# The first weight matrix moves to GpSimd's DMA queue, as one load, and the planner gives way to written order lists

## The chip, the cores and the metric

The kernel runs on one core of a Trainium2 chip. A core has five engines that run side by side, each through a program of its own: TensorE (matmuls and weight loads), VectorE, ScalarE, GpSimd and SyncE (here it only issues DMA transfers). They wait for one another by semaphores. Data come from HBM into SBUF by DMA; an engine that issues a DMA goes on with its program, and whoever needs the data waits for the DMA's semaphore. Matmul results go to PSUM. The metric is the device time of one execution in microseconds, the median of several runs.

## What is computed

An MLP mixer block over 2048 tokens of 512 features, in bfloat16:

```python
h = gelu(layernorm(x) @ w1)                  # x [2048, 512], w1 [512, 512]
# the four feature quarters of h are shifted along the tokens by +1, -1, +2, -2 (zeros come in)
hs = shifted(h) @ w2                         # w2 [512, 512]
x1 = x + hs
out = x1 + gelu(layernorm(x1) @ w3) @ w4     # w3 [512, 1792], w4 [1792, 512]
```

The layer normalizations have no learned scale; gelu is the tanh approximation.

## The kernel before

The tokens are 16 tiles of 128. All weights and activations stay in SBUF, so each is loaded once. For each tile `t` of layer 1: row statistics (either `bnst`/`bnag` on VectorE, lines 432 and 434, or two sums on ScalarE, lines 411 and 416), the reciprocal root `rstd` on GpSimd (line 439), the normalized rows into `xn_buf` (lines 448, 461, 470, 473), the transpose to `xnT` (on TensorE for the first tiles, line 506, with a copy out of PSUM on line 514; by a transposing DMA on SyncE's queue for the others, line 479), the first product with w1 (`up1`, line 642) and its gelu (line 657), the product with w2 (`mix`, line 697), whose shift is an offset in the columns of `hT`, and the addition to x (lines 709 and 713). Layer 2 then goes the same way with w3 (`up2`, line 642) and w4 (`down`, line 731), the last addition (line 739) and the store.

Tile 0 is special. Its rows are only centered (line 448, in two halves), transposed (line 506), and multiplied with w1 as rows (`rows0`, line 544, in two steps of two chunks of 128 features each); the gelu (line 585) applies the scale, and the result is transposed back (line 610). The first step, `rows0_0`, reads chunks 0 and 1 of w1, the second, `rows0_1`, chunks 2 and 3.

Before the first real matmul TensorE runs nine matmuls on zeros (line 756). ScalarE runs one small gelu (line 764) on the constant `eps_c`, ahead of its first row sum. GpSimd starts with eight small instructions that make constants (lines 364 to 374): the fixed columns of the statistics, the exponent for the reciprocal root, the identity matrix for the transposes, `eps_c`, and the zero edges of `hT`.

Every step is an `Op` with an engine, the resources that it reads and writes, and an estimated duration `dur`. TensorE's order is the string `SCRIPT`. `LOADS` is the order of the loads, all on SyncE; there w1 comes as two loads, `w1a` (chunks 0 and 1) and `w1b` (2 and 3), behind tiles 0-1 and 2 of x. For everything else, `order` works out due times from the durations, with corrections in `BIAS`, and `place` simulates the engines and the DMA rings to choose each engine's next step. `emit` then writes the programs in this order, with the semaphore waits that the resources ask for. Instructions up to the last one that the simulation starts before `ENTRY` are put ahead of the engines' wait in the start barrier.

Of the kernel before, what the change touches and what calls it, by code (L numbers as in the profile page):

```python
# [6 lines left out]
P = 128  # L7
# [7 lines left out]
class Op:  # L15


    def __init__(self, name, eng, fn, reads, writes, dur, queue):
        self.name, self.eng, self.fn = name, eng, fn
        self.reads, self.writes = list(reads), list(writes)  # L20
        self.dur, self.queue = dur, queue
        self.idx = 0
        self.descs = 8.0
        self.prio = 1e9
        self.first = None

class Program:

    HOP = {"pe": 200.0, "dve": 155.0, "act": 220.0, "pool": 120.0, "sp": 70.0}
    LOOK = {"dve": 300.0, "act": 300.0}
    DUE = 179877.0
    BEGIN = {"sp": 30.0, "act": 150.0, "pe": 400.0, "dve": 150.0, "pool": 450.0}
    ENTRY = 1900.0
    COLD, RESTART = 4300.0, 800.0
    RING = 150.0
    LAG = {"load": 750, "tp": 350}

    def __init__(self):  # L40
        self.ops = []
        self.lines = []

    def add(self, eng, name, fn, reads=(), writes=(), dur=100.0, queue=None):
        op = Op(name, eng, fn, reads, writes, dur, queue)
        op.idx = len(self.ops)
        self.ops.append(op)
        return op

    def line(self, names):  # L50

        self.lines.append(list(names))

    def order(self):
# [25 lines left out]
        order_only = set()  # L80
        for names in self.lines:
            for a, b in zip(names, names[1:]):
                assert named[a].eng == named[b].eng, (a, b)
                order_only.add((named[a].idx, named[b].idx))
        last = None
        pe_pos = 0
        for op in self.ops:
            if op.eng == "pe":
                if last is not None:
                    preds[op.idx].add(last.idx)  # L90
                last = op
                op.prio = pe_pos
                pe_pos += 1
        order_only = {(a, b) for a, b in order_only if a not in preds[b]}
        for a, b in order_only:
            preds[b].add(a)
        succs = [set() for _ in self.ops]
        for i, d in enumerate(preds):
            for j in d:
                succs[j].add(i)  # L100
        left = [len(s) for s in succs]
        stack = [i for i, n in enumerate(left) if n == 0]
        seen = 0
        while stack:
            i = stack.pop()
            seen += 1
            for j in preds[i]:
                if self.ops[j].eng != "pe":
                    self.ops[j].prio = min(self.ops[j].prio, self.ops[i].prio)
                left[j] -= 1  # L110
                if left[j] == 0:
                    stack.append(j)
        assert seen == len(self.ops), "cycle"
        if self.DUE:

            topo, left = [], [len(d) for d in preds]
            stack = [i for i, n in enumerate(left) if n == 0]
            while stack:
                i = stack.pop()
                topo.append(i)  # L120
                for j in succs[i]:
                    left[j] -= 1
                    if left[j] == 0:
                        stack.append(j)
            due, t = {}, self.DUE
            for op in self.ops:
                if op.eng == "pe" and not op.name.startswith("warm"):
                    due[op.idx] = t
                    t += op.dur
            for i in reversed(topo):  # L130
                op = self.ops[i]
                late = due.get(i, 1e9)
                for j in succs[i]:
                    o = self.ops[j]
                    hop = 70.0 if op.queue else (self.HOP[op.eng] if o.eng != op.eng else 120.0)
                    work = (2300.0 if op.queue == "tp" else op.dur + 1850.0) if op.queue else op.dur
                    late = min(late, o.prio - hop - work)
                op.prio = late
        for op in self.ops:
            op.prio += BIAS.get(op.name, 0.0)  # L140
            if op.first is not None:
                op.prio = op.first
        for names in self.lines:
            for a, b in reversed(list(zip(names, names[1:]))):
                named[a].prio = min(named[a].prio, named[b].prio - 1e-3)

        self.preds = preds
        out = self.place(succs, order_only)
        for a, b in order_only:
            preds[b].discard(a)  # L150
        return out

    def place(self, succs, order_only):

        npend = [len(d) for d in self.preds]
        ready = [0.0] * len(self.ops)
        cands = {e: [] for e in ENGINES}
        for op in self.ops:
            if npend[op.idx] == 0:
                cands[op.eng].append(op)  # L160
        free = dict(self.BEGIN)
        rings = {"sp": [], "act": []}
        fed = {}
        clock = moved = last = turned = self.total = 0.0
        out = []

        def finish(limit):
            nonlocal clock
            while True:
                heads = {e: r[0] for e, r in rings.items() if r}  # L170
                if not heads:
                    return None
                live = [e for e in heads if heads[e][0] <= clock]
                later = min([h[0] for h in heads.values() if h[0] > clock], default=1e18)
                if not live:
                    if later > limit:
                        return None
                    clock = later
                    continue
                first = min(live, key=lambda e: heads[e][1])  # L180
                step = heads[first][1] * len(live)
                ends = clock + step <= min(later, limit)
                if not ends:
                    step = min(later, limit) - clock
                for e in live:
                    heads[e][1] -= step / len(live)
                clock += step
                if ends:
                    return rings[first].pop(0)[2]
                if clock >= limit:  # L190
                    return None

        def release(op, o, at):
            npend[o.idx] -= 1
            if at is not None:
                ready[o.idx] = max(ready[o.idx], at)
            if npend[o.idx] == 0:
                cands[o.eng].append(o)

        def land(op):  # L200
            nonlocal moved, last, turned
            if op.queue == "tp":
                turned = max(clock + 500.0, op.start + 2450.0, last + 500.0, turned + 480.0)
                at = turned + self.LAG["tp"]
            elif op.name.startswith("out"):
                at = clock + 300.0
                self.total = max(self.total, at)
            else:
                moved += op.dur
                at = clock + 600.0 + min(600.0, 0.3 * moved) + (600.0 if op.dur > 1400.0 else 0.0)  # L210
                at += 50.0 if moved <= 1200.0 else self.LAG["load"] - 300.0 if moved <= 4000.0 else self.LAG["load"] if moved <= 11000.0 else self.LAG["load"] + 650.0
            if op.queue != "tp":
                last = max(last, at)
            op.landed = at
            for j in succs[op.idx]:
                if (op.idx, j) not in order_only:
                    release(op, self.ops[j], at + 30.0)

        while len(out) < len(self.ops):
            while True:  # L220
                best = None
                for e in ENGINES:
                    if cands[e]:
                        t = max(free[e], min(ready[o.idx] for o in cands[e]))
                        if best is None or t < best[0]:
                            best = (t, e)
                op = finish(best[0] if best else 1e17)
                if op is None:
                    break
                land(op)  # L230
            t, e = best
            look = self.LOOK.get(e, 1.0)
            op = min((o for o in cands[e] if ready[o.idx] <= t + look), key=lambda o: (o.prio, o.idx))
            cands[e].remove(op)
# [674 lines left out]
```

## Time and profile before

| | |
|---|---|
| median of 3 runs | 135.35 us (135.31 to 135.44) |
| span of the profiled execution | 133.7 us |
| what lies around the span (median less span) | 1.6 us |
| TensorE busy | 130.6 us, 98% of the span |
| TensorE's first real matmul (transposes of tile 0) | 4.24 us |
| first weight load of `rows0` | 5.40 us |
| loads from HBM | 6.82 MB |

The profiled execution's own time is its span, first to last instruction; the runs' time has the start and end of the program around it. In the profile a row of the timeline gives start, length, engine, line, operation, output and input, how many instructions were merged, and in brackets how long the engine was idle before and what ended that. PEld is TensorE's weight load, SPq the queue on which SyncE issues. A DMA issue's row is the time that the issuing engine spends on it; the transfer itself follows, and its time to landing is given by another view.

### The profile page before, as it was taken

Reading aid. Unit: us, or ns where it says so; the run is one execution under the profiler, and the core shown is the slowest. Engines: PE = TensorE matmul, PEld = TensorE weight load, DVE = VectorE, ACT = ScalarE, POOL = GpSimd, SP = SyncE. Lnnn points to the kernel's source line nnn. Section 1 sums busy time; section 2 is a strip of 40 time slices with the busy share of each in tenths; the row PEclk is TensorE's granted clock in tenths of the full one; section 3 lists DMA queues with packets and bytes.
Section 4 is the critical chain, followed back from the end, with each engine's and each line's share of the span. In section 5 each row is a group of like instructions: output and inputs, shape, how many; then the busy total and the mean of one; then the engine's idle time right before and its main releaser. Section 6 shows DMA issues by size and latency. Waiting matters only on the chain.

```text
span 133.7 us, 2004 instructions
## 1 busy us (share of the span) xinstructions
PE 130.6 (98%) x776; PEld 71.8 (54%) x789; DVE 50.9 (38%) x138; ACT 56.0 (42%) x89; POOL 30.9 (23%) x69
## 2 busy tenths in 40 slices
PE   8999999999999999999999999999999999999994
PEld 3488768874488444444444444444444444444464
DVE  1899998887550830052260003322220000232223
ACT  5699998858657155520025553000006663000000
POOL 2447567696544120012022003100000000000000
PEclk9999999999999999999999999999999999999999
DMA  4999966745442991002211000311111000111112
GB/s 134 329 349 401 237 150 95 83 89 107 98 99 49 295 329 40 0 0 43 77 42 39 0 0 0 78 39 44 39 42 37 0 0 0 39 44 39 39 39 78
DMA packets 21305, 12.19 MB, mean 91 GB/s; under 512 B 13872, under 2 KB 20784, under 8 KB 21296
## 3 DMA queue, kind: packets, MB, share of 16 engines
q1 hardware_dynamic: 20864, 11.93, 32.7%
q10 hardware_dynamic: 432, 0.13, 0.4%
q8 instruction: 6, 0.10, 0.3%
q14 instruction: 3, 0.02, 0.1%
HBM read 6.82 MB, written 2.10 MB: 67 GB/s over the span
## 4 chain that ended last, share of the span: by engine, by line
PE 94%; DMA 2%; DVE 2%; issue 1%; SPq 0%
PE y_ps L642 46%; PE o_ps L731 36%; PE o_ps L697 10%; DMA x_sb<-in_x_dram 2%; PE y_ps L506 1%; DVE st L432 1%; PE y_ps L544 1%; DVE xn_buf L448 0%; DVE xn_buf L461 0%; DVE o_sb L739 0%; PE o_ps L610 0%; DVE mv L434 0%; SPq L894 0%
## 5 line engine op out<-in xcount | busy, mean ns | idle before, releaser
L642 PE MATMUL y_ps<-xnT,w_sb 128*128 128x512 bf16 (+2 forms) x421 | 63.6, 308 | 0.2
L642 PEld LDWEIGHTS y_ps<-xnT,w_sb 128*128 128x128 bf16 x424 | 38.4, 98 | 24.6 <-DVE mv L434 0.2
L731 PE MATMUL o_ps<-w_sb,h2T 128*128 128x512 bf16 (+3 forms) x248 | 48.7, 355 | 0.2
L657 ACT ACTIVATE h2T<-y_ps 128x1024 bf16<-128x1024 f32 (+1 forms) x29 | 28.6, 993 | 47.2 <-PE y_ps L642 47.1
L731 PEld LDWEIGHTS o_ps<-w_sb,h2T 128*128 128x128 bf16 x252 | 23.6, 98 | 25.2
L739 DVE TENSOR_TENSOR o_sb<-o_ps,x_sb 128x512 bf16<-128x512 f32 (+3 forms) x18 | 11.4, 632 | 45.7 <-PE o_ps L731 45.7
L439 POOL TENSOR_TENSOR rstd<-mv,neghalf 128x1 f32<-128x1 f32 x20 | 11.1, 553 | 35.1 <-DVE mv L434 30.1
L697 PE MATMUL o_ps<-w_sb,hT 128*128 128x512 bf16 x58 | 14.8, 379 | 0.3
L432 DVE BATCH_NORM_STATS2 st<-x_sb 128x6 f32<-128x512 bf16 x20 | 13.5, 676 | 2.6 <-DMA x_sb<-in_x_dram 2.5
L713 DVE TENSOR_TENSOR x_sb<-o_ps,x_sb 128x512 bf16<-128x512 f32 x10 | 6.8, 677 | 14.8 <-PE o_ps L697 14.8
L439 POOL TENSOR_TENSOR rstd<-vpe,neghalf 128x1 f32<-128x1 f32 x12 | 6.7, 558 | 15.6 <-DVE vpe L428 15.5
L473 POOL TENSOR_SCALAR xn_buf<-x_sb,rstd,nmr 128x512 bf16<-128x512 bf16 x12 | 9.2, 764 | 1.0 <-DVE nmr L466 0.4
L657 ACT ACTIVATE hT<-y_ps 128x512 bf16<-128x512 f32 (+1 forms) x10 | 8.1, 806 | 3.1 <-PE y_ps L642 2.9
L697 PEld LDWEIGHTS o_ps<-w_sb,hT 128*128 128x128 bf16 x64 | 6.1, 98 | 5.7
L709 DVE SCALAR_TENSOR_TENSOR x_sb<-o_ps,x_sb 128x512 bf16<-128x512 f32 x6 | 4.1, 681 | 12.1 <-PE o_ps L697 12.1
L416 ACT ACTIVATE junk<-x_sb 128x512 bf16<-128x512 bf16 x12 | 7.5, 622 | 2.1 <-DVE x_sb L709 2.0
L461 DVE TENSOR_SCALAR xn_buf<-x_sb,mv,rstd 128x512 bf16<-128x512 bf16 x13 | 6.1, 471 | 2.7 <-POOL rstd L439 2.0
L470 ACT ACTIVATE xn_buf<-x_sb,nmr,rstd 128x512 bf16<-128x512 bf16 x6 | 4.9, 813 | 0.5 <-POOL nmr L466 0.4
L756 PE MATMUL o_ps<-zeros 128*128 128x512 bf16 x9 | 4.0, 631 | 0.4 <-DVE zeros L363 0.4
L411 ACT ACTIVATE junk<-x_sb 128x512 bf16<-128x512 bf16 x6 | 3.7, 624 | 1.2 <-DMA x_sb<-in_x_dram 1.2
L434 DVE BATCH_NORM_AGGREGATE mv<-st 128x2 f32<-128x9 f32 x20 | 3.8, 192 | 0.3
L506 PE MATMUL y_ps<-ident,xn_buf 128*128 128x128 bf16 x32 | 3.4, 236 | 0.2 <-DVE xn_buf L461 0.2
(34 smaller groups left out, 28.7 us busy)
## 6 DMA issues: line engine op xcount, KB each, us to landing
out_dram<-o_sb SPq DMA_DIRECT2D x15, 128.0 KB, 1.7
w_sb<-in_w_dram SPq DMA_DIRECT2D x1, 1792.0 KB, 10.9
w_sb<-in_w_dram SPq DMA_DIRECT2D x2, 896.0 KB, 6.2
x_sb<-in_x_dram SPq DMA_DIRECT2D x4, 256.0 KB, 3.6
w_sb<-in_w_dram SPq DMA_DIRECT2D x4, 256.0 KB, 4.3
x_sb<-in_x_dram SPq DMA_DIRECT2D x5, 128.0 KB, 4.5
x_sb<-in_x_dram SPq DMA_DIRECT2D x1, 384.0 KB, 5.7
xnT<-xn_buf SPq DMA_TRANSPOSE x24, 2.5
```

What stands on the lines that cost most here:

```text
L416: (lambda d: (lambda e: e.activation(d, src, ACT_F.Square, accum_out=sums[:, q, 1:2])))(junk[:, b, :]),
L432: pg.add("dve", f"bnst{q}", lambda e: e.bn_stats(st9[:, q, 0:6], src), reads=rs, writes=[(("st", q), 0)], dur=605)
L439: lambda e: e.tensor_tensor(col(rstd), var, neghalf[:], ALU.pow),
L461: lambda e: e.tensor_scalar(dst, src, mv[:, q, 0:1], rstd[:, q : q + 1], ALU.subtract, ALU.mult),
L470: f = lambda e: e.activation(dst, src, ACT_F.Identity, bias=nmr[:, q : q + 1], scale=rstd[:, q : q + 1])
L473: f = lambda e: e.tensor_scalar(dst, src, rstd[:, q : q + 1], nmr[:, q : q + 1], ALU.mult, ALU.add)
L642: ins = e.matmul(y_ps[:, p, W * i : W * (i + 1)], wsb[:, dc, P * fc : P * (fc + 1)], src[:, dc, P * t0 : P * t0 + W], start=(dc == 0), sto ...
L657: (lambda d, s: (lambda e: e.activation(d, s, ACT_F.Gelu_apprx_tanh)))(dst, ysrc),
L697: ins = e.matmul(dst, hT[:, j, c0 : c0 + P], w2_sb[:, j, :], start=(j == order[0]), stop=(j == order[-1]))
L713: f = lambda e: e.tensor_tensor(x1_sb[:, t, :], dst, x_sb[:, t, :], ALU.add)
L731: ins = e.matmul(dst, h2T[:, fc, P * t : P * (t + 1)], w4_sb[:, fc, cs], start=(fc == 0), stop=(fc == FC - 1))
L739: (lambda d, c: (lambda e: e.tensor_tensor(o_sb[:, oi, c], d, x1_sb[:, t, c], ALU.add)))(dst, cs),
```

## The change

w1 becomes one load, issued by GpSimd as the first instruction of its program, ahead of the eight constants. The other loads stay on SyncE in the same order. The planner goes (durations, `BIAS`, due times and the simulation), and `ORDER` lists the steps of SyncE, ScalarE, VectorE and GpSimd by name; `SCRIPT` still gives TensorE's. `AHEAD` names the instructions in front of the wait in the start barrier; it holds those of the kernel before with w1 as one, and the loads of x tiles 3 and 4-5 besides. With one load there is one semaphore for w1, so `rows0_0` waits for all four chunks. The diff, cut (the lists to their beginnings; removed durations left out):

```diff
-BIAS = {"bnag16": -989.166, "nmr10": 207.118, "rstd14": 756.261, "rstd5": 886.138, "ssq1": -15, ...}
 LOADS = """
-x0-1 x2 tp2 w1a w1b x3 x4-5 w2b w2a tp5 x6 tp6 x7 x8-10 tp4 w3 x12-13 tp0 x11 tp17 x14-15 tp26 tp5 w4a tp3
-w4b
+x0-1 x2 w1@pool x3 x4-5 w2b w2a x6 x7 x8-10 w3 x12-13 x11 x14-15 w4a w4b
 """
+W2FIRST = "b"
+AHEAD = "zeros trip0 trip1 neghalf ident0 epsc pad0 ident1 pad1 warm_gelu warm1 dma_w1 dma_x0 dma_x2 dma_x3 dma_x4".split()
...
+ORDER = {
+    "sp": """
+dma_x0 dma_x2 dma_x3 dma_x4 dma_w2b dma_w2a dma_x6 dma_x7 dma_x8 dma_w3 dma_x12 dma_x11 tp16 tp17 dma_x14 tp9
...
+    "act": """
+warm_gelu sum0 ssq0 ev0_0 ev0_1 ev1act gelur0 sum5 gelu1_1_0 ssq5 gelu1_2_0 sum7 ev3 norm5 ssq7 gelu1_3_0 sum9
...
+    "dve": """
+zeros bnst1 bnag1 norm0_0 norm0_1 bnst2 norm1 bnag2 msq0 vpe0 norm2 ev1dve bnst3 ev2 bnag3 bnst4 evh0 norm3
...
+    "pool": """
+dma_w1 trip0 trip1 neghalf ident0 epsc pad0 ident1 pad1 rstd1 rstd2 rstd0 rstd3 rstd4 rstd5 nmr5 rstd6 nmr6
...
         named = {op.name: op for op in self.ops}
...
+        lists = {e: [named[n] for n in ORDER[e].split()] for e in ENGINES if e != "pe"}
+        lists["pe"] = [op for op in self.ops if op.eng == "pe"]
...
+        at = dict.fromkeys(ENGINES, 0)
+        done, out = set(), []
         while len(out) < len(self.ops):
...
+            heads = [lists[e][at[e]] for e in ENGINES if at[e] < len(lists[e])]
+            heads = [op for op in heads if preds[op.idx] <= done]
+            op = min(heads, key=lambda op: (op.name not in AHEAD, ENGINES.index(op.eng)))
+            at[op.eng] += 1
+            done.add(op.idx)
             out.append(op)
...
-        if op.start < prog.ENTRY:
+        if op.name in AHEAD:
             ahead = len(listed)
```

## The prediction

> **What bounds the kernel now.** I read the busy times first, then the chain of work that ended last, then the instructions in order of time for the first 7 us, then the DMA transfers there.
>
> The busy line, from the page:
>
> ```profile
> PE 130.6 (98%) x776; PEld 71.8 (54%) x789; DVE 50.9 (38%) x138; ACT 56.0 (42%) x89; POOL 30.9 (23%) x69
> ```
>
> TensorE is busy for 130.6 of 133.7 us, so a change elsewhere counts only where it moves TensorE. The chain says where that can be (start, length, what; in us):
>
> ```profile
> 0.08 2.77 DMA x_sb<-in_x_dram
> ...
> 2.87 0.70 DVE st L432
> ...
> 3.60 0.20 DVE mv L434
> 3.80 0.36 DVE xn_buf L448 x2
> 4.15 0.60 DVE st L432
> 4.75 0.33 DVE xn_buf L461
> ...
> 5.12 0.49 PE y_ps L506 x4
> 5.62 0.86 PE y_ps L544 x4
> 6.48 0.22 PE y_ps L506 x4
> ```
>
> The reader should see two parts. Up to 5.12 the chain is the landing of the first load of x and then VectorE's first normalizations. From 5.12 (the transposes of token tile 1) it is TensorE without a break, to the last addition at 131.96. So the first 5.4 us are the only place where the order of loads can decide, and any lateness of TensorE there goes to the end in full, as nothing later has slack to give it back. w1 is not in this chain. How near it is to it, the instructions in order of time show:
>
> ```profile
> 0.08 0.95 SPq L384 DMA_DIRECT2D x_sb<-in_x_dram  x2
> 0.71 0.17 POOL L369 MEMSET st<- 128x64 f32 x1 [0.29 <-POOLq L894]
> 1.08 0.95 SPq L393 DMA_DIRECT2D w_sb<-in_w_dram  x2
> 2.16 0.85 SPq L384 DMA_DIRECT2D x_sb<-in_x_dram  x2
> 2.87 0.69 DVE L432 BATCH_NORM_STATS2 st<-x_sb 128x6 f32<-128x512 bf16 x1 [2.50 <-DMA x_sb<-in_x_dram]
> 5.40 0.58 PEld L544 LDWEIGHTS y_ps<-w_sb,xnT 128*128 128x128 bf16 x4
> ```
>
> (Line three is the two halves of w1.) They are issued at 1.08 and about 1.56. The issues with their time to landing, of the stretches 1.0 to 1.4 and 2.0 to 2.4 us, give 3.7 and 4.0 us for them:
>
> ```profile
> w_sb<-in_w_dram SPq DMA_DIRECT2D x1, 256.0 KB, 3.7
> ...
> w_sb<-in_w_dram SPq DMA_DIRECT2D x1, 256.0 KB, 4.0
> ```
>
> So they land at about 4.8 and 5.5. The first is used at 5.40, the second two matmuls of 0.216 us (0.86 over 4) later, its weights at about 5.7. Slack: 0.6 and 0.2 us. Last, the DMA traffic by half microseconds (the last three columns are granted TensorE clock, DMA share, GB/s):
>
> ```profile
> 1.50:2.00 0.50, 0.50 (x2) 0.15 (x1) 0.00 (x0) 0.20 (x1) 0.19 (x2) 1.00 0.54 190
> 2.00:2.50 0.50, 0.50 (x2) 0.15 (x1) 0.00 (x0) 0.00 (x0) 0.00 (x0) 1.00 1.09 383
> 2.50:3.00 0.50, 0.50 (x3) 0.19 (x2) 0.13 (x1) 0.13 (x1) 0.00 (x0) 1.00 0.34 94
> 3.00:3.50 0.50, 0.50 (x3) 0.23 (x2) 0.50 (x1) 0.50 (x2) 0.00 (x0) 1.00 0.61 158
> 4.50:5.00 0.50, 0.38 (x4) 0.11 (x1) 0.50 (x3) 0.30 (x2) 0.00 (x0) 1.00 1.09 371
> ```
>
> When full, the engines move some 375 GB/s. Between the first loads of x and w1 there is a hole of about 1 us, and VectorE is idle from 0.37 to 2.87.
>
> **The base of the sum.** The profiled span is 133.7 us, the median of the runs 135.35, so 1.6 us lie around the span. The profiled execution has no time of its own beyond that; I add differences in the span to 135.35. A time within 0.2% (0.27 us) is about what a measurement of this kernel can't tell from no change.
>
> **The change, part by part.**
>
> The order lists. Read against the instructions in order of time, each list names the order that the trace has, engine by engine, with w1 as the one difference. The matmul order is the same, only written out. Term: 0.
>
> SyncE. It loses two issues, 1.08 to 2.03. The third load of x, at 2.16 before, moves to about 1.1, and every later load about 1.0 us forward; two of them now stand ahead of SyncE's wait in the start barrier, which cost at most 0.1 us (the gap from 2.03 to 2.16). This earns nothing: the statistics of token tile 3 start at 6.37 right behind a copy, without idle time, and TensorE has no wait on a load after 5.12. But it fills the time in which w1 had the DMA engines nearly alone: these loads now run beside it.
>
> GpSimd. Its program begins with the issue of w1 and then has the eight instructions that ran from 0.71 to 1.69. The trace has no DMA issued by GpSimd, so the time G that it holds the engine is bounded: from the shortest plain issue on SyncE, 0.38, to the longest transposing one, 2.27. [...] Who waits behind it: the epsilon constant (done 1.13) gates ScalarE's first activation (0.20 us), which must be out of the way by 2.87; with G = 1.0 it ends near 2.35. The identity (done 1.63) is wanted at 4.07, the constants of the statistics (done 0.96) at 3.60, the first reciprocal root at 3.88. Term: 0 at G = 1.0; at 2.27 the activation would end near 3.6, push the first row sum by 0.7, and with it the centering at 3.71 and all of the chain: +0.7. Below nothing it can't be, since none of these gates the chain now.
>
> w1 itself. All four chunks now have one completion, which the first weight load at 5.40 waits for; before, only half had to be there. When does it land? GpSimd can issue at about 0.6 (its first instruction behind the barrier is at 0.71). Plus G = 1.0, plus 0.95 from issue to the first bytes as for the first load of x (issued 0.08, bytes from about 1.0): bytes from about 2.55. From there SyncE's ring has x2's rest, x3, x4-5 and a half of w2 behind one another without a pause, so I give w1 half of 375 GB/s: 524 KB in 2.8 us, to 5.35. Last bytes to landing: x2's bytes are through at about 2.8 and it landed near 3.15 (issued 0.59, 2.6 to landing), so 0.35: landing at 5.7, against 5.40. Term: +0.35 us, with the dispatch. Behind that weight load stands all of TensorE's program, in order, so all of it moves. The gap is of the size of the one before the transposes of tile 1 (4.87 to 5.12, VectorE), after which the matmuls ran at 0.216 us all the same, so I add nothing for a slower TensorE. Bounds: at best it behaves like the first load of x (2.8 us to landing for 256 KB) plus 262 KB more at full rate (0.7), from 0.6: landing 4.1, term 0. At worst G is 2.27, the first bytes take w1a's time (1.08 to about 2.9, 1.8 us), half rate, and the 0.35: landing near 7.8, term +2.4. I stay near the middle because the issue is early and the share is what is surely lost.
>
> [...]
>
> x. w1's bytes may start before the first load of x is through (2.85). From 2.0 on that load has little left (383 GB/s until 2.5, shared with x2), so with bytes at 2.55 the term is 0; from 1.6, some 180 KB of it are left (127 GB/s from 1.0 to 1.5, then 190), which at half rate take 0.95 instead of 0.5 us: +0.45.
>
> Sum: 0 + 0 + 0 + 0.35 + 0 = **+0.35 us: 135.7**.
>
> [...]
>
> **The rivals.**
>
> *A: w1 lands in time and nothing else moves.* It needs first bytes by about 2.2 at half share, or more than half a share. For it: the hole between 2.5 and 3.5 us, in which w1 could run nearly alone, and the slack of G. Against it: SyncE's ring no longer has that hole to offer if x3 follows x2 at once. Time 135.35, within 0.27. [...]
>
> *C: w1 starts too well or holds GpSimd too long.* The first takes x's share (+0.45) the second delays the first row sum (decides from G about 1.5, +0.1 to +0.7). The chain begins with x's landing, so this goes through in full: about 135.8. Against it: half the rate only for the last part of x, and 1.2 us between ScalarE's first activation and its need.
>
> *D: faster.* The one way: the first load of x lands earlier. Between 1.5 and 2.0 the engines were half used (190 GB/s), just after the issue of w1's first half on the same queue. If preparing w1 there caused that hole, its loss lets 95 KB more through in that half microsecond, and x lands up to 0.25 us sooner; TensorE starts as much earlier, the rest being a chain of fixed lengths: 135.1. It decides when the hole of 1.5 to 2.0 closes. Against it: another load is issued in the same place (x3 for w1a), and w1's bytes want the same engines.
>
> **How the numbers follow.** B, the forecast (w1 late by more than 0.27): 0.41, since its middle lies only just past the deadline. A: 0.30, as w1's landing has bounds on both sides of 5.40. C: 0.17. D: 0.12, half of its price being within the bound. Slower 0.41 + 0.17 = 0.58, same 0.30, faster 0.12. The likeliest is B at 135.7; its own range is 135.6 to 136.6. For 8 in 10 the range reaches down to 135.1, which takes in A and D's price, and up to 136.7 (+1.35), which leaves out the upper part of w1's bounds.
>
> **What would show it.** B: the first weight load of the row product (L544) starts at about 5.75 instead of 5.40, its idle time ended by a DMA of w1, and everything behind it keeps its lengths. A: it stays at 5.40, w1 landing before. C: the first statistics start after 2.87, or ScalarE's first sum is ended by GpSimd. D: they start before 2.87. The GpSimd row of the issue gives G. I would be wrong most if GpSimd's descriptors take several us or if w1 gets far more than half of the engines.

## The result and the profile after

The change makes the kernel slower: 1.0068 of the time before, 95% interval 1.0041 to 1.0095, which is +0.92 us, from 135.35 to about 136.3. Executions more than 1.5% above the fastest of their kernel are left out of every ratio here and below; in this result they are three of the five, 139.25 to 139.91 us, and what they lose is the subject of the experiments.

The profiled execution took 136.28 us and has a span of 135.0 us, 1.3 us longer than the span before. The runs say 0.92 probably because the profiled execution of the kernel before was a good one: in later runs of that kernel the time is some 1.3 us more than the span (135.32 against 134.0, for one), so its 133.7 belonged to a time near 135.0, not 135.35.

The busy times of the kernel after, from the page:

```profile
PE 131.3 (97%) x789; PEld 71.7 (53%) x789; DVE 51.1 (38%) x138; ACT 56.0 (41%) x89; POOL 31.9 (24%) x70
```

TensorE works nearly as long as before. (13 more of its matmuls are in the records; the number of weight loads is the same.) What changed is the beginning of the chain that ended last (start, length, what):

```profile
0.60 0.02 POOLq L711
0.62 0.61 issue
1.23 5.41 DMA w_sb<-in_w_dram
6.64 0.05 issue
6.68 1.04 PE y_ps L377 x4
7.72 0.22 PE y_ps L340 x4
7.94 0.89 PE y_ps L473 x16
```

The chain no longer starts with x and VectorE. It starts with GpSimd's issue of w1 at 1.23 and goes through its landing at 6.64 into the row product (L377 here, L544 before). Its end is at 7.72 instead of 6.48, and the transposes behind it take 0.22 us as before. The instructions in order of time show the same from the waiting side:

```profile
0.08 1.92 SPq L220 DMA_DIRECT2D x_sb<-in_x_dram  x4
1.23 0.95 POOL L229 DMA_DIRECT2D w_sb<-in_w_dram  x1 [0.80 <-POOLq L711]
...
2.65 0.20 ACT L593 ACTIVATE warm<-eps_c 128x1 f32<-128x1 f32 x1 [1.17 <-POOL hT L209]
2.89 0.69 DVE L267 BATCH_NORM_STATS2 st<-x_sb 128x6 f32<-128x512 bf16 x1 [2.52 <-DMA x_sb<-in_x_dram]
...
5.15 0.40 PE L340 MATMUL y_ps<-ident,xn_buf 128*128 128x128 bf16 x4 [0.27 <-DVE xn_buf L295]
6.68 0.55 PEld L377 LDWEIGHTS y_ps<-w_sb,xnT 128*128 128x128 bf16 x4 [1.31 <-DMA w_sb<-in_w_dram]
6.68 1.04 PE L377 MATMUL y_ps<-w_sb,xnT 128*128 128x512 bf16 x4 [1.14 <-DMA w_sb<-in_w_dram]
```

The first statistics start at 2.89 (2.87 before) and the transposes of tile 1 at 5.15 (5.12): x is not delayed. Then the first weight load of the row product stands at 6.68 where it stood at 5.40. That is 1.28 us, and the span grew by 1.3. The small activation that waits for GpSimd's constant starts at 2.65 and ends at 2.85, just before ScalarE's first sum starts at 2.89. The one view left is the DMA traffic by half microseconds (last three columns: granted TensorE clock, DMA share, GB/s):

```profile
2.00:2.50 0.50, 0.50 (x2) 0.15 (x1) 0.00 (x0) 0.00 (x0) 0.50 (x5) 1.00 1.12 391
2.50:3.00 0.50, 0.50 (x3) 0.19 (x2) 0.11 (x1) 0.31 (x2) 0.33 (x4) 1.00 1.15 143
3.00:3.50 0.50, 0.50 (x3) 0.23 (x2) 0.50 (x1) 0.50 (x2) 0.17 (x2) 1.00 0.39 14
3.50:4.00 0.50, 0.50 (x3) 0.04 (x1) 0.47 (x4) 0.50 (x3) 0.10 (x1) 1.00 0.68 225
4.00:4.50 0.50, 0.50 (x5) 0.36 (x4) 0.50 (x2) 0.23 (x2) 0.48 (x1) 1.00 1.08 418
```

Between 3.0 and 3.5 the engines move 14 GB/s, though by then the third load of x (issued at 1.09) and w1 (issue row over at 2.18) are both waiting to be moved. The packets of w1, 128 of 4096 bytes, begin at 3.89 and end at 6.05.

### The profile page after: what moved, and what is told of

Read it like the earlier page. It is cut to its first block, busy times and chain, and to the rows that moved or that the text cites. A ratio compares the mean times of both kernels' runs of the same rounds, so it can differ in the third digit from the quotient of the medians.

```text
span 135.0 us, 2015 instructions
## 1 busy us (share of the span) xinstructions
PE 131.3 (97%) x789; PEld 71.7 (53%) x789; DVE 51.1 (38%) x138; ACT 56.0 (41%) x89; POOL 31.9 (24%) x70
## 4 chain that ended last, share of the span: by engine, by line
PE 94%; DMA 4%; issue 1%; DVE 0%; POOLq 0%
PE y_ps L473 46%; PE o_ps L561 36%; PE o_ps L527 10%; DMA w_sb<-in_w_dram 4%; PE y_ps L340 1%; PE y_ps L377 1%; DVE o_sb L569 0%; PE o_ps L442 0%; POOLq L711 0%
## 5 line engine op out<-in xcount | busy, mean ns | idle before, releaser
L527 PE MATMUL o_ps<-w_sb,hT 128*128 128x512 bf16 x64 | 15.8, 379 | 0.0
L300 POOL TENSOR_SCALAR nmr<-mv,rstd 128x1 f32<-128x1 f32 x13 | 3.4, 266 | 0.8
```

The lines of the kernel that those rows point to most:

```text
L527: ins = e.matmul(dst, hT[:, j, c0 : c0 + P], w2_sb[:, j, :], start=(j == order[0]), stop=(j == order[-1]))
```

## The experiments

All but one edit the changed kernel, so its line numbers hold throughout; `f0` runs it as it is. Lists that an edit doesn't touch are left out, and so are the names in `AHEAD` that move along with a load. The kernel before, run beside them, took 135.37 to 135.55 us (medians; three single executions of it took 174 to 281 us).

### What part of the change costs: one load on SyncE

The theory is that w1 is late because it comes through GpSimd's queue beside SyncE's loads; among the rivals are the single completion and the new order lists. The first kernel keeps the one load and the lists, and puts w1 back on SyncE behind tile 2 of x.

```diff
-x0-1 x2 w1@pool x3 x4-5 w2b w2a x6 x7 x8-10 w3 x12-13 x11 x14-15 w4a w4b
+x0-1 x2 w1 x3 x4-5 w2b w2a x6 x7 x8-10 w3 x12-13 x11 x14-15 w4a w4b
...
-dma_x0 dma_x2 dma_x3 dma_x4 dma_w2b ...
+dma_x0 dma_x2 dma_w1 dma_x3 dma_x4 dma_w2b ...
...
-dma_w1 trip0 trip1 neghalf ...
+trip0 trip1 neghalf ...
```

> The changed kernel with w1 as one load, but on SyncE in its old place behind x2; lists and TensorE's order as in the changed kernel. Theory (GpSimd's queue is what makes w1 late, by its long way from issue to first bytes): w1 lands near 5.5 us, where its second half landed before, the row product starts at 5.5 to 5.6 instead of 5.40, and the time is 135.5 (135.35 to 135.6). Rival 1 (one completion for all four chunks is the cost): the row product starts after 6.0, time 136 or more. Rival 2 (the written lists or the two loads more ahead of the barrier cost): 136.3 as in the changed kernel.

Measured: 135.6 (ten runs, 135.46 to 138.58), ratio 1.0006 (0.9994 to 1.0017). In the instructions in order of time the row product follows the transposes of tile 1:

```profile
5.26 0.61 PE L340 MATMUL y_ps<-ident,xn_buf 128*128 128x128 bf16 x4 [0.39 <-DVE xn_buf L295]
5.90 1.16 PE L377 MATMUL y_ps<-w_sb,xnT 128*128 128x512 bf16 x4
```

The whole of w1 landed between 5.03 and 5.85, just as the transposes of tile 1 were over (5.87), and the matmuls follow without idle time. The transposes take 0.61 us here and 0.40 in the changed kernel's profile; with 0.40 they would have been over near 5.66, and w1 waited for by 0.2 us (an estimate). In the times, one completion instead of two costs nothing that can be measured. Two of the ten executions, 137.63 and 138.58, are long with one queue too; their recorded mean clock, 0.987 and 0.988, is like that of the split on GpSimd below (0.988). They have no trace.

### The lists alone

w1 as two halves on SyncE, as before the change; what is left of the change is the written-out order.

```diff
-x0-1 x2 w1@pool x3 x4-5 ...
+x0-1 x2 w1a w1b x3 x4-5 ...
...
-dma_x0 dma_x2 dma_x3 dma_x4 ...
+dma_x0 dma_x2 dma_w1a dma_w1b dma_x3 dma_x4 ...
...
-dma_w1 trip0 trip1 neghalf ...
+trip0 trip1 neghalf ...
```

> The changed kernel with w1 back in two halves on SyncE, so that only the written lists differ from the kernel before. Theory and rival 1: 135.35 within 0.1, the row product at 5.40. Rival 2 (the lists cost): 135.7 to 136.3.

Measured: 135.53 (ten runs, 135.12 to 136.31), ratio 0.9999 (0.998 to 1.0018). The lists cost nothing that can be measured. What is left is w1 on GpSimd.

### Two halves on GpSimd

```diff
-x0-1 x2 w1@pool x3 x4-5 ...
+x0-1 x2 w1a@pool w1b@pool x3 x4-5 ...
...
-dma_w1 trip0 trip1 neghalf ...
+dma_w1a dma_w1b trip0 trip1 neghalf ...
```

> The changed kernel with w1 in two halves, both first in GpSimd's program. Theory: first bytes near 3.9 as for the one load, the first half landing near 5.5 and the second near 6.6; the first step of the row product starts near 5.6, the second waits until 6.6 instead of 5.8; the time is 136.1 (135.9 to 136.4), at most 0.3 better than the changed kernel. Rival 1 (one completion is the cost): the split gives the loss back, 135.4 to 135.6. A second issue of 1 us on GpSimd would delay the constants, and ScalarE's first row sum by up to 0.8 us.

Measured: 139.74 (four runs, 139.49 to 140.03), ratio 1.0312 (1.0282 to 1.0342). That is far from what was expected. The two issues take 0.91 and 0.73 us, from 1.24 on, and the halves land at 6.85 and 8.82. In order of time:

```profile
6.90 0.60 PE L377 MATMUL y_ps<-w_sb,xnT 128*128 128x512 bf16 x2 [0.84 <-DMA w_sb<-in_w_dram]
...
8.87 1.03 PE L377 MATMUL y_ps<-w_sb,xnT 128*128 128x512 bf16 x2 [1.37 <-DMA w_sb<-in_w_dram]
```

The second pair takes 1.03 us, the first 0.60. The busy times by stretch say why (third column from the end, the granted clock):

```profile
7.00:8.50 1.50, 0.50 (x2) 0.01 (x1) 0.58 (x1) 0.00 (x0) 0.00 (x0) 1.00 1.07 344
8.50:12.00 3.50, 3.13 (x24) 2.58 (x25) 1.09 (x3) 1.30 (x3) 0.55 (x1) 0.51 1.07 386
12.00:14.00 2.00, 1.95 (x27) 1.53 (x26) 1.55 (x6) 1.93 (x5) 0.75 (x2) 1.00 1.02 402
```

After the two waits TensorE is granted half its clock, by the records from 8.54 to 11.96. So the late w1 cost twice here: the waits of 0.84 and 1.37 us, and some 3.4 us at half speed.

### w1 first on ScalarE's queue

To see whether it is GpSimd or any second queue: ScalarE issues w1, first in its program.

```diff
-x0-1 x2 w1@pool x3 x4-5 ...
+x0-1 x2 w1@act x3 x4-5 ...
...
-warm_gelu sum0 ssq0 ...
+dma_w1 warm_gelu sum0 ssq0 ...
...
-dma_w1 trip0 trip1 neghalf ...
+trip0 trip1 neghalf ...
```

> The changed kernel with the one load of w1 first in ScalarE's program instead of GpSimd's: still a second queue beside SyncE's, sharing the same DMA engines, but not GpSimd's. Theory: w1 lands before 5.4 and the row product starts at 5.4 unless x is late; 135.35 to 135.7, the upper end if w1's bytes hold up the first load of x by up to 0.4 us. Rival 3 (any second queue makes w1 late, since it gets only its share beside SyncE's loads): w1 lands after 6.0, time 136 or more.

Measured: 136.39 (ten runs, 135.87 to 137.88), ratio 1.0096 (1.0052 to 1.014). In order of time:

```profile
0.21 0.44 ACTq L229 DMA_DIRECT2D w_sb<-in_w_dram  x1
...
5.34 0.69 DVE L267 BATCH_NORM_STATS2 st<-x_sb 128x6 f32<-128x512 bf16 x1 [1.02 <-DMA x_sb<-in_x_dram]
6.41 0.40 PE L340 MATMUL y_ps<-ident,xn_buf 128*128 128x128 bf16 x4 [1.74 <-DVE xn_buf L295]
6.64 1.03 PE L377 MATMUL y_ps<-w_sb,xnT 128*128 128x512 bf16 x4
```

The issue at 0.21 brings w1 in by 4.94, in time. But now tile 2 of x, issued at 0.60, lands at 5.32, where it landed near 3.15; VectorE stands 1.02 us, and the row product begins at 6.64, where the changed kernel has it at 6.68. The loss has changed sides: the time is that of rival 3, for another reason than its late w1. This is the first mechanism of the prediction's rival C, with the second load of x as the one that suffers. The wait of 1.74 us in front of the transposes leaves TensorE's speed as it was (1.03 us for the row product).

### The changed kernel again

Two theories of the executions near 139.5 stand against each other in this run and the next: that the time in which TensorE stands idle costs them speed, or that it has nothing to do with them.

> The changed kernel once more, as the yardstick of the next one. Either theory: its undisturbed executions at 136.3 to 136.5, others near 139.5.

Measured: six runs, 137.69 to 140.69, median 139.8 against 135.5; none is near 136.3. The profile is of an execution of 140.12. Its chain:

```profile
1.23 6.88 DMA w_sb<-in_w_dram
8.11 0.05 issue
8.16 1.89 PE y_ps L377 x4
10.05 0.43 PE y_ps L340 x4
10.47 1.71 PE y_ps L473 x16
12.18 0.44 PE o_ps L442 x4
```

w1 ends at 8.11 instead of 6.64. Of its 16 parts twelve have landed by 6.34; the last four come at 6.91, 7.03, 7.27 and 8.11. By the packets it is the data that is late: the last ten of the 128 end between 6.33 and 7.69. The rest of the loss is speed. From the row product to the transposes of the gelu (L442) the matmuls take 4.46 us (8.16 to 12.62), in the execution of 136.28 it was 2.38 (6.68 to 9.06): everything has half the rate. The wait is 1.48 us longer and the half rate adds 2.08, together 3.6; the spans differ by 3.8. But it isn't the wait that put TensorE to half rate here:

```profile
0.43 4.02 PE L586 MATMUL o_ps<-zeros 128*128 128x512 bf16 x9 [0.43 <-DVE zeros L199]
...
5.13 0.61 PE L340 MATMUL y_ps<-ident,xn_buf 128*128 128x128 bf16 x4 [0.25 <-DVE xn_buf L295]
8.16 1.89 PE L377 MATMUL y_ps<-w_sb,xnT 128*128 128x512 bf16 x4 [2.42 <-DMA w_sb<-in_w_dram]
```

The matmuls on zeros start 0.43 us apart, twice the 0.216 of later ones, as they do at the start of every trace here. In the execution of 136.28 TensorE had left the half rate by the transposes of tile 1 (0.40 us); here they take 0.61, so it still had it when the wait began, and it keeps it until 13.0. (The clock records of this profile begin only there, so before that its granted clock reads 1.00; the durations show the half rate.)

### A short filler

Four matmuls on zeros between the transposes of tile 1 and the row product.

```diff
-warm:9 sa:0 sb:0 ty:1 ra:0 rb:0 ...
+warm:9 sa:0 sb:0 ty:1 warm:4 ra:0 rb:0 ...
```

> The changed kernel with four more matmuls on zeros (512 columns each) between the transposes of tile 1 and the row product, in the time in which TensorE waits for w1. Nothing else changes, and their result is not used. [...] Rival (the executions near 139.5 have nothing to do with the idle time): as many near 139.5 as in the changed kernel.

Measured: six runs, 136.39 to 139.77, median 139.28. Four of the six lie near 139.5 (139.16 to 139.77), much as the rival has it. But w1 landed at 8.38 here, TensorE still stood idle for 2.03 us behind the filler, and the clock was at half from 8.29 to 11.70. The filler was too short to tell anything about the clock.

### SyncE's further loads held back

If w1 is late because SyncE's loads run beside it, it must come earlier when they don't. The third load of x, and so everything behind it on SyncE, waits for w1.

```diff
-                             writes=[(("x", t), 0) for t in range(t0, t1)], queue=eng)
+                             reads=[(("w1", 0), 0)] * (t0 == 3), writes=[(("x", t), 0) for t in range(t0, t1)], queue=eng)
```

> The changed kernel in which SyncE issues its third load (x3) and all behind it only once w1 has landed, so that w1 has the DMA engines to itself behind x0-1 and x2. Later tiles come late, so only w1's landing is read from it, not the time. Theory (GpSimd's path sets the first bytes, 2.7 us behind the issue): first bytes near 3.9 as before, 524 KB at 375 KB/us, landing near 5.9 instead of 6.64, so that sharing is 0.7 of the lateness. Rival 3 (sharing is the cost): landing at 5.4 or before.

Measured: one execution, 138.03. In order of time:

```profile
5.97 1.04 PE L377 MATMUL y_ps<-w_sb,xnT 128*128 128x512 bf16 x4 [0.37 <-DMA w_sb<-in_w_dram]
...
8.03 0.70 DVE L267 BATCH_NORM_STATS2 st<-x_sb 128x6 f32<-128x512 bf16 x1 [1.50 <-DMA x_sb<-in_x_dram]
```

w1 has landed by 5.92, all parts within 0.7 us, and the wait falls from 1.14 to 0.37. The total is no better because the held loads of x now come late (the second line). The landing is the theory's 5.9, and not as early as rival 3's 5.4: of the 1.24 us by which w1 came behind 5.40 in the execution of 136.28, 0.72 goes with SyncE's loads. But the reason given for it didn't hold: the first packets of w1 begin at about 2.9 here, so the 3.89 of the changed kernel is no fixed time from the issue, and the last ends at 5.47, so the bytes take 2.5 us even without the other loads.

### The constants before w1

```diff
-dma_w1 trip0 trip1 neghalf ident0 epsc pad0 ident1 pad1 rstd1 ...
+trip0 trip1 neghalf ident0 epsc pad0 ident1 pad1 dma_w1 rstd1 ...
```

> The changed kernel with w1 behind the eight constants in GpSimd's program instead of ahead of them. Theory (a fixed way of about 2.7 us from GpSimd's issue to the first bytes): issue 0.5 to 1.0 us later than 1.23, first bytes 4.4 to 4.9, landing 7.1 to 7.6, the row product and the span later by as much. Rival 4 (the first bytes near 3.9 are set by the pause that all DMA queues show from 2.75 to 3.5, not by GpSimd): first bytes and landing where they were, within 0.2.

Measured: one execution, 140.6. The issue (0.95 us) is at 1.86, 0.63 later than at the head of the program, and w1 lands at 8.20. The row product starts at 8.25 after 2.64 us of idle time. The clock line of the page (40 slices of 3.5 us) has two slices at half:

```profile
PEclk9955999999999999999999999999999999999999
```

The first packets begin at 4.70, as the theory had it, so rival 4 falls. But the landing is later than the theory's 7.6 and hardly later than in the execution of 140.12 (8.11), though the issue is 0.63 later: between these two executions it is not the time of the issue that sets when the last part is there.

### ScalarE at GpSimd's time

w1 is issued by ScalarE behind its first small activation, about when GpSimd issues it.

```diff
-x0-1 x2 w1@pool x3 x4-5 ...
+x0-1 x2 w1@act x3 x4-5 ...
...
-warm_gelu sum0 ssq0 ...
+warm_gelu dma_w1 sum0 ssq0 ...
...
-dma_w1 trip0 trip1 neghalf ...
+trip0 trip1 neghalf ...
```

> w1 as one load on ScalarE's queue, but behind ScalarE's first activation, so that it is issued near 1.7 us, as late as GpSimd issued it in the run with the constants first (1.86, landing 8.2). Theory (GpSimd's own way of making descriptors is what makes the load late): w1 lands at least 0.7 us earlier than there, by 6.6 to 7.4, and the time is 136.2 to 137. Rival 5 (any load issued that late beside SyncE's queue comes that late): landing 7.7 to 8.7, time 138 or more.

Measured: 140.08 (four runs, 139.43 to 140.26), ratio 1.0327 (1.0294 to 1.036). In order of time:

```profile
1.17 0.43 ACTq L229 DMA_DIRECT2D w_sb<-in_w_dram  x1
...
8.40 1.89 PE L377 MATMUL y_ps<-w_sb,xnT 128*128 128x512 bf16 x4 [2.63 <-DMA w_sb<-in_w_dram]
```

The issue is at 1.17 rather than the 1.7 expected, and still w1 lands at 8.36. The theory that GpSimd's own path makes w1 late falls: a queue of ScalarE that starts at that time is as late. Here it isn't a few parts that lag. w1's packets, of 1024 bytes like SyncE's, run from 2.76 to 7.88, and from 4 to 7 us w1 gets 0.43 of the 0.92 MB moved: about the half share of the prediction.

### One half on each queue

`w1a` on SyncE behind tile 2, `w1b` on GpSimd first.

```diff
-x0-1 x2 w1@pool x3 x4-5 ...
+x0-1 x2 w1a w1b@pool x3 x4-5 ...
...
-dma_x0 dma_x2 dma_x3 dma_x4 ...
+dma_x0 dma_x2 dma_w1a dma_x3 dma_x4 ...
...
-dma_w1 trip0 trip1 neghalf ...
+dma_w1b trip0 trip1 neghalf ...
```

> The first half of w1 on SyncE, third as in the kernel before, the second half first on GpSimd. Theory: the first step of the row product starts near 5.4 again; the second half, 256 KB from GpSimd, lands near 6 (half the bytes of the one load at the same share), and the second step waits some 0.2 to 0.5 us: 135.6 to 136.0. If GpSimd's lateness depends on size alone: 135.35. If not at all on size: second half at 6.6, 136.2.

Measured: ten runs from 135.68 to 140.24, median 137.24, ratio 1.0061 (1.0027 to 1.0095). Two of the ten lie within the 135.6 to 136.0 of the theory. In the profile (an execution of 138.4) GpSimd's half has landed by 6.75, and SyncE's, which landed at 5.12 when both halves were on SyncE, has parts from 3.50 to 7.10, against 3.86 to 5.12 there. With two queues at work, parts of the loads on either of them came late.

### A filler that is long enough

```diff
-warm:9 sa:0 sb:0 ty:1 ra:0 rb:0 ...
+warm:9 sa:0 sb:0 ty:1 warm:12 ra:0 rb:0 ...
```

> The changed kernel with twelve more matmuls on zeros between the transposes of tile 1 and the row product (2.6 us at full clock, to about 8.0), their result unused. Theory (executions near 139.5 are a landing of w1 near 8.1 plus 1.7 us of half clock, earned by the idle time before): TensorE is never idle long enough, all executions end at 137.7 to 138.4, better than the usual ones of the changed kernel and worse than its best. Rival (the half clock has another cause): executions near 139.5 to 140 remain.

Measured: 137.9 (four runs, 137.55 to 138.8), ratio 1.0197 (1.015 to 1.0244). In order of time:

```profile
5.34 2.75 PE L586 MATMUL o_ps<-zeros 128*128 128x512 bf16 x12
...
7.95 1.04 PE L377 MATMUL y_ps<-w_sb,xnT 128*128 128x512 bf16 x4
```

w1 lands at 7.90, nearly as late as in the runs near 140, and the row product takes 1.04 us, not 1.89; the granted clock is full from 4.01 us, where its records begin. Against the execution of 140.12 the row product is 0.21 us earlier and the time 2.57 less. The times spread a little wider than expected, but none is near 139.5. So the second loss is the clock, and keeping TensorE busy takes it away. It doesn't give back the wait.

### ScalarE at GpSimd's time, SyncE held

The run with ScalarE again, with SyncE's third load of x held until w1 is there.

```diff
-                             writes=[(("x", t), 0) for t in range(t0, t1)], queue=eng)
+                             reads=[(("w1", 0), 0)] * (t0 == 3), writes=[(("x", t), 0) for t in range(t0, t1)], queue=eng)
```

> The run with w1 issued by ScalarE behind its first activation (landing 8.36), now with SyncE's third load and all behind it held until w1 has landed. Later tiles come late, so the end is late for that too, as in the run with GpSimd and the same hold (138.0). New theory (two queues with work at once is what makes w1 late, whichever engine issues it): w1 lands at 5.0 to 5.9, the row product starts by 6.0, the time is 137.5 to 138.5 in all executions. Rival (a load issued that late on a second queue is late by itself): landing after 7, time over 139.5.

Measured: 137.49 (four runs, 137.26 to 138.66), ratio 1.0171 (1.0131 to 1.0212). The page gives the time from issue to landing:

```profile
w_sb<-in_w_dram ACTq DMA_DIRECT2D x1, 512.0 KB, 4.6
```

It was 7.2 us without the hold. The landing (5.81) and the wait before the row product, 0.30 us instead of 2.63, are as the theory had them; the times are a little wider. With GpSimd as the issuer the same hold brought the time to landing to 4.7 us, from 5.4 to 7.2 without it. Held, w1 lands at 5.81 and 5.92, as one load on SyncE did at 5.85. For both issuers, then, it is the other queue's work at the same time that makes w1 later than that run had it (one profile with the hold for each). No run with a second queue was faster than the kernel before, and from ScalarE w1's landing took 2.6 us more beside SyncE's loads than without them (7.2 against 4.6).

No kernel here beats the one before: the two with w1 back on SyncE equal it.

## Why the prediction was right, and where it was not

**The mechanism: right.** B was forecast and B is what the trace shows: the weight load of the row product late, its idle time ended by w1, the lengths behind it unchanged, x on time. So it is in the profiled execution; in that of 140.12 the lengths behind it are not unchanged, and the 2.1 us that this costs are in no term of the forecast.

**The size: 0.35 forecast, 0.92 in the ratio.** Its terms of w1's landing, one by one. The issue was put at 0.6 and is at 1.23 (+0.63); GpSimd's constants began at 0.71 there, but its load doesn't begin as early. G was put at 1.0, a value between its two bounds for which no run shows a reason; GpSimd's issue row is 0.95. From the issue row's end to the first bytes I gave 0.95, and it is 1.71 (2.18 to 3.89), +0.76: the pause of all queues at 3.0 to 3.5 was in the trace of before as the hole between 2.5 and 3.5, and I took it to be room that SyncE's loads would fill, which they didn't. The transfer was to take 2.8 us at half the engines and takes 2.16: while both queues were busy w1 got about four fifths of the bytes (94 KB against 22 from 4.25 to 4.5). On ScalarE's queue the half share is what w1 did get. From the last packet to the landing I gave 0.35, and it is 0.59 (6.05 to 6.64). The differences, +0.63 - 0.05 + 0.76 - 0.64 + 0.24, make 0.94, from 5.7 to 6.64. Three terms were too small, and the share that I called surely lost made its own too large; the forecast came as near as it did partly because they cancel, which is luck.

**What the sum has no term for: the spread.** The range's upper end, 136.7, holds the ratio's 136.3 but none of the executions at 137.7 to 140.7, which is where this kernel was in nine of its eleven. I gave w1 a rate, as if its 16 parts ended together. In the execution of 140.12 twelve do, and four come 0.6 to 1.8 us later; in the run with the short filler four come 1.4 to 2.2 us later. They pass even the upper bound that I had for w1's landing, 7.8 (8.11 in the execution of 140.12), and I had left the upper part of those bounds out of the range.

**The clock: a term at nothing that fails in the long executions.** I added nothing for a slower TensorE, because behind a gap of 0.25 us the matmuls ran at 0.216 us "all the same". The trace of before shows something else there:

```profile
0.43 4.02 PE L756 MATMUL o_ps<-zeros 128*128 128x512 bf16 x9 [0.43 <-DVE zeros L363]
...
5.45 1.03 PE L544 MATMUL y_ps<-w_sb,xnT 128*128 128x512 bf16 x4
```

TensorE starts at half rate (its matmuls on zeros begin 0.43 us apart, those of the row product 0.216), and by the trace's clock records it went over to the full rate at 5.37 us, in the middle of the transposes behind that gap. The time differs between executions: about 6.4 in the run of the lists alone, whose row product therefore ends 0.48 us later (span 134.2 against 133.7). In the profiled execution after the change the zero held, since TensorE had its full rate before the wait of 1.14 us (0.40 us for the transposes of tile 1) and kept it (0.22 for those behind the row product). In the execution of 140.12 and in the run with ScalarE at GpSimd's time it didn't have it yet when the wait began, and got it only at 13.0: 2.1 us of loss in the first. In the split on GpSimd, the short filler, the constants first and one half on each queue it had it and lost it again, for 3.4 us, with the constants first for 6.8. There the 3.4 us before the loss held 2.1 to 2.3 us of idle time in all. Up to 1.94 us in all in 3.4 us (SyncE held, GpSimd), or one wait of 1.74 us (ScalarE first), came without a loss. In the split on GpSimd and with the short filler the half rate lasted 3.42 and 3.41 us (8.54 to 11.96, and 8.29 to 11.70), and in as long a time before it TensorE had worked for 1.1 and 1.3 us.

**The zero terms: right.** The order lists (0.9999), SyncE's earlier loads, and GpSimd's hold of its engine: the first activation ended by 2.85, before 2.89, though with 0.04 us to spare instead of the half microsecond forecast. In the run with two issues in front of the constants that margin is gone and the transposes of tile 0 start at 4.63 instead of 4.24.

**The rivals.** A (in time) fell. D (x sooner) fell: x landed at 2.87, in the place of 2.85. C didn't happen in the changed kernel, but the run with ScalarE first shows that it is real: w1 half a microsecond ahead of need and x2 two microseconds late. No issue time between the two was tried.

**What stays open.** Why the queues pause near 3 us; why single parts are late by up to 2 us when two queues run, and which; whether it is whole DMA engines that fall behind (with the short filler, four parts of the following load of w2 on SyncE are late too, 8.49 to 9.31 where the other twelve are there by 7.33); what made the two long executions with w1 on SyncE; why GpSimd's load starts half a microsecond later than its constants would. That the half rate goes with the idle time rests on the filler's four executions and its one trace. Why the full rate came only at 13.0 in two traces is not shown; nor is whether it is the idle time in all that counts: 1.94 us of it in 3.4 us came without a loss, 2.1 us with one.

## What to carry to other kernels

A load that is needed early gains nothing here by another engine's issuing it: beside the other queue's bytes it came late (at 6.64 to 8.82 us, for a need at 5.40), and ahead of them it held up what was first (tile 2 of x at 5.32 instead of 3.15). One queue in the order of need was the best that any run here found (135.53 and 135.6 us). Judge a load by the landing of its last part against its need, over several executions, not by the mean rate. And where TensorE may wait in front of its first real work, look in the trace at the rate that it has before the wait and behind it: waits of 1.48 us and more in front of the row product came with half rate in all five traces that have one, one of 1.74 us in front of tile 1's transposes did not. Matmuls on zeros until the data was there took that part away here (1.04 us for the row product instead of 1.89).

## What the runs showed of the hardware

- The issue of a 512 KB load held GpSimd for 0.95 us, those of two of 256 KB for 0.91 and 0.73; ScalarE took 0.43 for the same 512 KB. GpSimd's load moved in packets of 4096 bytes of 0.159 us, those of SyncE and ScalarE in packets of 1024 bytes of 0.046 us. Beside SyncE, GpSimd's load got about four fifths of the bytes (94 KB against 22 in a quarter of a microsecond) and ScalarE's about half (0.43 of 0.92 MB).
- After the first loads the queues stood nearly still for half a microsecond in the execution of 136.28 (14 GB/s from 3.0 to 3.5, with work waiting on both). The same half microsecond had 158 GB/s before the change, 78 in the execution of 140.12, and 338 with w1 first on ScalarE's queue: there was no pause there.
- With two queues at work w1's 16 parts landed within 0.6 us of one another in the execution of 136.28, within 2.1 in that of 140.12, within 3.2 from ScalarE; with SyncE held within 0.7 and 1.0. As one load on SyncE they took 0.8. The changed kernel's times lie between 136.28 and 140.69 us.
- TensorE ran at half rate from the start of every execution traced (0.43 us between matmuls of 512 columns, 0.216 later) and reached the full rate between 3.7 and 6.4 us, or at 13.0 in two traces with a long wait.
